# Sampled blocks of two batches counted through: full sets across a batch border, whole rows of two batches in one group

## The chip, the cores and the metric

The kernel runs on one core of a Trainium2 chip. The metric is the device time of one execution in microseconds (us), the median over several runs; lower is better.

## The reference

Block-sparse attention for 4 batches, 8 heads, 768 positions and a head width of 64, in blocks of 32 positions (24 blocks a batch), followed by a feed-forward with 512 inputs, 2048 hidden values and 512 outputs on all 3072 tokens. All numbers are float32.

```python
scores = scale * np.matmul(q, k.transpose(0, 1, 3, 2))
mask = np.abs(blk_i - blk_j) <= window                       # window = 1
mask = mask | (blk_i == 0) | (blk_j == 0) | (blk_i == n_blocks - 1) | (blk_j == n_blocks - 1)
for qb in range(n_blocks):
    for kb in sampled_blocks[qb]:                            # 3 blocks
        mask[qb*block:(qb+1)*block, kb*block:(kb+1)*block] = True
scores = np.where(mask, scores, -1e9)
attn = softmax(scores); x = attn @ v                         # x: tokens x 512
h = x @ w_in
out = (np.maximum(h, 0) + np.log1p(np.exp(-np.abs(h)))) @ w_out
```

So the query blocks 1 to 22 of a batch see at most eight key blocks: three neighbours, the first, the last, and three sampled ones. The query blocks 0 and 23 see all 24. The former are called sampled blocks here, the latter whole rows. The list of sampled blocks is the same for all batches.

## The kernel before

**Sets.** The attention works on sets of four query blocks (128 rows). The 24 blocks of a batch are taken in the order 1 to 23, then 0, and cut into six groups. Groups 0 to 4 hold 20 sampled blocks and are full sets. Group 5 holds the sampled blocks 21 and 22 and the whole rows 23 and 0; it is worked as two sets, first the whole rows (a "whole set"), then the two sampled blocks (a "half set", `ni = 2`). A batch has seven sets, the kernel 28. Each set has two units, of four heads each.

**A unit.** `scores` multiplies queries with gathered keys on TensorE (L579 for sampled blocks, one 64x32 corner of the array per block; L603 for whole rows) and adds the mask and takes the minimum on VectorE (L585, L610). `exponents` runs on ScalarE (L635). `transposes` turns the weights on TensorE (L648) and copies them out of PSUM (L653 VectorE, L655 ScalarE). `products` multiplies with the values (L687, L701). At the end of a set `normalise` divides by the sums (L717), and `turn`, `x_high` and `x_low` transpose the result and split it into a high and a low part for the feed-forward (L732, L746, L750). A set's output takes one of the 24 places of 128 tokens; three places make a tile of the feed-forward, eight tiles in all.

**Keys and values.** `kT` holds the keys of one batch in a single buffer. `gather_keys` copies from it into one of two buffers `kg`: the neighbours with one VectorE copy (L498), the first and last block with two ScalarE copies where the buffer still has those of another batch (L481), the sampled ones with three copies a block, on GpSimd apart from the first set (L512). After the scores of a batch's whole set, `score_piece` lets the remaining gathers of that batch be issued and asks for the next batch's keys (`load_kT`, four DMAs on SP's queue); gathers from the new keys follow three pieces later (`BEHIND`). The values come into one of two buffers: near ones by a DMA on SP's queue (L542), sampled ones by an indirect DMA a block from GpSimd (L545). Queries are loaded two groups ahead (`load_queries`, L448).

**Order.** Each unit is cut into two pieces, `score_piece` and `transpose_piece`, software-pipelined over units: scores run two units ahead of the values. There are 116 pieces. `needs` (L841) says how many of them must be done before tile t of the feed-forward can start: 15, 31, 43, 59, 71, 87, 99, 116. The first 15 run alone; after that `between` and `due` spread the others over the feed-forward's steps so that each tile's need is met half a step early.

**Feed-forward.** It runs in 128 steps (`hidden`, `project`), each with 12 matmuls of 384 columns (L238 to L240) and 9 of 512 (L296 to L298). In the first 48 steps all eight tiles meet the first six of sixteen slices of the weights; in the last 80 steps they meet the other ten. The attention lies beside the first 42 steps. Beside it `convert` also turns the 64-bit weights into 32-bit ones, in ticks that go by pieces and steps (ScalarE L156, L160; VectorE L166 to L183). `store` adds up and writes the output (L321 to L326).

Of the kernel before, what the change touches and what calls it, by code (L numbers as in the profile page):

```python
# [19 lines left out]
BLOCK = 32  # L20
# [30 lines left out]
def sparse_attention_ffn(  # L51
    ctx: ExitStack,
    tc: tile.TileContext,
    q: bass.AP,
    k: bass.AP,
# [20 lines left out]
    B, NG, P, NP, NI, _ = q.shape  # L76
    NB = k.shape[2]
# [16 lines left out]
    order = [(b, g) for b in range(B) for g in range(NG)]  # L94
    place = {bg: n for n, bg in enumerate(order)}
# [215 lines left out]
    def store(phase, t):  # L311
        for m in range(GROUPS):
            n = t * GROUPS + m
            b, g = order[n]
# [7 lines left out]
            lo = b * S + (4 * g + 1) * BLOCK  # L322
            n = P if g < NG - 1 else P - BLOCK
            nc.sync.dma_start(out=out[lo : lo + n], in_=os_[0:n])
            if n < P:
                nc.sync.dma_start(out=out[b * S : b * S + BLOCK], in_=os_[n:P])  # L326
# [7 lines left out]

    blk = ac.tile([P, NB * NR * 2], I32, name="blk")
    rf = ac.tile([P, NB, NR], F32, name="rf")
    pkf = ac.tile([1, NB], F32, name="pkf")
# [5 lines left out]
    ixf = ac.tile([P, NB], F32, name="ixf")  # L343
    ix = ac.tile([P, B, NB], I32, name="ix")
    mask = ac.tile([P, NG, NS], F32, name="mask")
    iu = ac.tile([P, NG], I32, name="iu")
    iuf = ac.tile([P, NG], F32, name="iuf")
    rp = ac.tile([P, NG, NR], F32, name="rp")
    hit = ac.tile([P, NG, NR], F32, name="hit")
    tmp = ac.tile([P, NG, NR], F32, name="tmp")  # L350
    zero = ac.tile([P, 1], F32, name="zero")
    nc.gpsimd.memset(zero, 0.0)
    for i in range(NI):
        nc.gpsimd.iota(
            iu[i * BLOCK : (i + 1) * BLOCK], pattern=[[NI, NG]], base=1 + i, channel_multiplier=0
        )
# [13 lines left out]
    nc.vector.memset(rp, 0.0)  # L370
# [34 lines left out]
    def make_mask():  # L405
        nc.vector.tensor_copy(out=iuf, in_=iu)

        for i in range(NI):
            rows = slice(i * BLOCK, (i + 1) * BLOCK)
            n = NG if i < 2 else NG - 1  # L410
            nc.vector.tensor_copy(out=rp[rows, 0:n], in_=rf[rows, 1 + i : 2 + i + NI * (n - 1) : NI, :])

        nc.vector.tensor_tensor(
            out=tmp, in0=rp, in1=iuf.unsqueeze(2).to_broadcast([P, NG, NR]), op=ALU.subtract
# [14 lines left out]
        nc.vector.memset(mask[0:BLOCK, 0, 0:1], NEG)  # L429
        nc.vector.memset(mask[BLOCK : 2 * BLOCK, NG - 1, 2:3], NEG)  # L430
# [12 lines left out]
    def load_queries(m):  # L443
        if m >= len(order):
            return
        b, g = order[m]
        qc[b, g] = wk.tile([P, NP, NI, BLOCK], F32, tag="qc", name=f"qc{b}_{g}", bufs=2)
        nc.sync.dma_start(out=qc[b, g], in_=q[b, g])  # L448
# [23 lines left out]
    def load_keys(*ms):  # L472

        wanted.extend(m for m in ms if m < len(order))
        while wanted and order[wanted[0]][0] in kT and not waiting:
            gather_keys(wanted.pop(0))

    def end_keys(m, copies):

        for copy, slot, blkno in zip(copies, (NR, 2 * NR + 1), (0, LAST)):  # L480
            copy(  # L481
                out=kg[m % 2][:, :, slot, :],
                in_=kT[order[m][0]][:, blkno : blkno + 1, :].to_broadcast([P, NI, NP * BLOCK]),
            )

    def gather_keys(m):
        b, g = order[m]
        ni = NI if g < NG - 1 else 2
        kd = kg[m % 2]

        def of_block(i):

            eng = (nc.vector if i < 2 else nc.scalar) if m == 0 else nc.gpsimd
            copy = nc.scalar.copy if m == 0 and i >= 2 else eng.tensor_copy
            if i == 0:
                at = kT[b][:, 4 * g : 4 * g + NR, :]
# [480 lines left out]
```

## Time and profile before

| | |
|---|---|
| median of 3 runs | 806.67 us (806.6 to 806.96) |
| profiled execution | 800.52 us, span of its instructions 798.7 us |
| TensorE matmul busy | 770.1 us, 96% of the span |
| TensorE weight loads busy | 645.6 us, 81% |
| VectorE busy | 536.4 us, 67% |
| ScalarE busy | 545.5 us, 68% |
| GpSimd busy | 188.2 us, 24% |
| DMA | 137.78 MB, mean 173 GB/s |

Busy times are averages over stages that have different limits, so they are read by stage below. TensorE's rows overlap, because matmuls are pipelined and small ones run beside each other; what a burst of them costs is read from the time at which it starts and the one at which the next work starts.

### The profile page before, as it was taken

Reading aid. Unit: us, or ns where it says so; the run is one execution under the profiler, and the core shown is the slowest. Engines: PE = TensorE matmul, PEld = TensorE weight load, DVE = VectorE, ACT = ScalarE, POOL = GpSimd, SP = SyncE. Lnnn points to the kernel's source line nnn. Section 1 sums busy time; section 2 is a strip of 40 time slices with the busy share of each in tenths; the row PEclk is TensorE's granted clock in tenths of the full one; section 3 lists DMA queues with packets and bytes.
Section 4 is the critical chain, followed back from the end, with each engine's and each line's share of the span. In section 5 each row is a group of like instructions: output and inputs, shape, how many; then the busy total and the mean of one; then the engine's idle time right before and its main releaser. Section 6 shows DMA issues by size and latency. Waiting matters only on the chain.

```text
span 798.7 us, 21332 instructions
## 1 busy us (share of the span) xinstructions
PE 770.1 (96%) x8108; PEld 645.6 (81%) x8108; DVE 536.4 (67%) x1379; ACT 545.5 (68%) x1306; POOL 188.2 (24%) x358
## 2 busy tenths in 40 slices
PE   8779999999999999999999999999999999999997
PEld 7556677777778777778788998899889988998896
DVE  5799999776878768776656864546454645455554
ACT  3798986867868678777667866555655565556553
POOL 6762955217345145442000000000000000000000
PEclk9999999999999999999999999999999999999999
DMA  7799787666767866857215922222130403021021
GB/s 289 274 349 348 256 295 272 236 232 234 288 229 271 311 252 221 282 165 260 97 41 185 355 81 79 80 77 83 34 125 1 146 14 139 20 107 53 0 80 41
DMA packets 42663, 137.78 MB, mean 173 GB/s; under 512 B 5248, under 2 KB 5376, under 8 KB 38080
## 3 DMA queue, kind: packets, MB, share of 16 engines
q1 hardware_dynamic: 35152, 112.15, 39.1%
q0 software_dynamic: 7120, 23.34, 8.0%
q8 instruction: 64, 1.05, 0.5%
q10 hardware_dynamic: 288, 0.93, 0.3%
q14 instruction: 39, 0.32, 0.1%
HBM read 105.98 MB, written 30.41 MB: 171 GB/s over the span
## 4 chain that ended last, share of the span: by engine, by line
PE 69%; DVE 12%; ACT 12%; issue 3%; DMA 2%; SPq 0%; POOL 0%; DVEq 0%; POOLq 0%; ACTq 0%
PE h L238 10%; PE o L296 10%; PE o L298 9%; PE o L297 9%; PE h L239 9%; PE h L240 9%; ACT pr L635 5%; PE x L687 3%; PE s L579 3%; PE t L648 3%; DVE pr L585 2%; PE warm L816 2%; DMA kT<-in_k_dram 2%; ACT pt L655 1%; DVE wt L179 1%
## 5 line engine op out<-in xcount | busy, mean ns | idle before, releaser
L253 DVE SCALAR_TENSOR_TENSOR e<-u,e 128x384 f32<-128x384 f32 x128 | 71.4, 558 | 177.3 <-ACT u L251 177.2
L238 PE MATMUL h<-x,w 128*128 128x384 f32 x512 | 178.3, 348 | 4.5 <-DVE nmax L610 2.5
L239 PE MATMUL h<-x,w 128*128 128x384 f32 x512 | 172.8, 338 | 0.0
L240 PE MATMUL h<-x,w 128*128 128x384 f32 x512 | 172.6, 337 | 0.0
L296 PE MATMUL o<-w,gh 128*128 128x512 f32 x384 | 156.0, 406 | 0.0
L297 PE MATMUL o<-w,gh 128*128 128x512 f32 x384 | 151.6, 395 | 1.2 <-issue 1.2
L298 PE MATMUL o<-w,gl 128*128 128x512 f32 x384 | 152.1, 396 | 0.0
L635 ACT ACTIVATE pr<-pr,nmax 128x256 f32<-128x256 f32 (+2 forms) x208 | 110.1, 531 | 59.4 <-DVE nmax L585 43.0
L244 ACT ACTIVATE e<-h 128x384 f32<-128x384 f32 x128 | 62.4, 488 | 117.3 <-PE h L240 117.3
L545 POOL DMA_INDIRECT vg<-in_v_dram,ix x88 | 92.0, 1046 | 117.0 <-PE x L687 90.8
L512 POOL COPY kg<-kT 128x128 f32 x252 | 93.1, 418 | 86.8 <-PE s L579 80.1
L238 PEld LDWEIGHTS h<-x,w 128*128 128x128 f32 x512 | 96.1, 188 | 19.3 <-DVE nmax L610 4.5
L239 PEld LDWEIGHTS h<-x,w 128*128 128x128 f32 x512 | 96.3, 188 | 4.9 <-issue 0.4
L240 PEld LDWEIGHTS h<-x,w 128*128 128x128 f32 x512 | 96.1, 188 | 0.0
L298 PEld LDWEIGHTS o<-w,gl 128*128 128x128 f32 x384 | 72.1, 188 | 19.0 <-issue 1.8
L268 ACT CAST gh<-u 128x384 fp32r<-128x384 f32 x128 | 65.6, 512 | 25.1 <-PE o L297 25.1
L296 PEld LDWEIGHTS o<-w,gh 128*128 128x128 f32 x384 | 72.1, 188 | 12.3 <-issue 0.8
L297 PEld LDWEIGHTS o<-w,gh 128*128 128x128 f32 x384 | 72.2, 188 | 10.7
L274 DVE TENSOR_TENSOR gl<-u,gh 128x384 fp32r<-128x384 f32 x128 | 70.6, 552 | 7.5 <-ACT gh L268 6.8
L585 DVE CUSTOM_DVE_ANT_1 pr<-s,mask 128x256 f32<-128x256 f32 (+1 forms) x192 | 70.0, 415 | 5.5 <-PE s L579 5.4
L259 ACT ACTIVATE u<-u 128x384 f32<-128x384 f32 x128 | 67.0, 523 | 9.3 <-DVE e L253 8.6
L254 DVE SCALAR_TENSOR_TENSOR e<-h,e 128x384 f32<-128x384 f32 x128 | 70.8, 553 | 2.7
(81 smaller groups left out, 1046.7 us busy)
## 6 DMA issues: line engine op xcount, KB each, us to landing
vg<-in_near_dram SPq DMA_DIRECT2D x19, 1024.0 KB, 5.3
xD<-x SPq DMA_DIRECT2D x8, 1536.0 KB, 6.0
x<-xD SPq DMA_DIRECT2D x8, 1536.0 KB, 7.3
raw<-in_w_in_dram SPq DMA_DIRECT2D x16, 512.0 KB, 7.2
raw<-in_w_out_dram SPq DMA_DIRECT2D x16, 512.0 KB, 9.3
qc<-in_q_dram SPq DMA_DIRECT2D x24, 256.0 KB, 6.1
vg<-in_v_dram SPq DMA_DIRECT2D x12, 512.0 KB, 6.5
yD<-os SPq DMA_DIRECT2D x24, 256.0 KB, 3.0
```

The source lines that it names most:

```text
L238: nc.tensor.matmul(ph, wh[:, cols], hi[:, c], start=(c == 0), stop=False)
L239: nc.tensor.matmul(ph, wh[:, cols], lo[:, c], start=False, stop=False)
L240: nc.tensor.matmul(ph, wl[:, cols], hi[:, c], start=False, stop=(c == NC - 1))
L253: nc.vector.scalar_tensor_tensor(out=e, in0=u, scalar=-1.0, in1=e, op0=ALU.add, op1=ALU.subtract)
L254: nc.vector.scalar_tensor_tensor(out=e, in0=ph, scalar=0.0, in1=e, op0=ALU.max, op1=ALU.subtract)
L296: nc.tensor.matmul(po[m], gh[:, cols], wh, start=first, stop=False)
L297: nc.tensor.matmul(po[m], gh[:, cols], wl, start=False, stop=False)
L298: nc.tensor.matmul(po[m], gl[:, cols], wh, start=False, stop=last)
L512: copy(out=kd[:, i, 1 + NR + s, :], in_=kT[b][:, bass.ds(x, 1), :].rearrange("p n f -> p (n f)"))
L545: nc.gpsimd.indirect_dma_start(out=vd[:, 1, i, :], out_offset=None, in_=v, in_offset=bass.IndirectOffsetOnAxis(ap=ix[:, b, 4 * g + 1 + i : ...
L585: nc.vector.tensor_tensor_reduce(out=pr[r][rows, j], in0=ps[r][rows, j], in1=mask[rows, g].unsqueeze(2).to_broadcast([ni * BLOCK, NS, BLOCK]),
L635: nc.scalar.activation(x, x, AF.Exp, bias=nmax[rows, r, j : j + 1], scale=-1.0, accum_out=rs[rows, h : h + 1])
```

## The change

The 22 sampled blocks of a batch are no longer cut into five and a half sets. The 88 sampled blocks of all batches are counted through in order and cut into 22 full sets; there is no half set any more. In each pair of batches (11 sets) the sixth set holds the blocks 21 and 22 of the first batch and 1 and 2 of the second.

- Whole rows stay one set a batch, but have their queries in an input of their own (`ends`) and stand now ahead of the fifth and the eleventh sampled set of a pair. Their normalised rows go to a tile `xe` that holds both batches; they are turned together, after the second one, and take one place of 128 tokens (`WHOLE`). There are 26 sets, 52 units, 108 pieces; `needs` becomes 15, 31, 43, 55, 67, 83, 95, 108.
- The keys of the middle set are gathered in two parts, one from each batch's keys. The first and last key block are copied for those block rows whose batch has changed (`stale`).
- The masks are made for the 11 sets of a pair instead of the 6 groups of a batch; since a set may have blocks of two batches, the block numbers are written for eight runs of blocks (`seams`) instead of four.
- The small tiles of the start lie in `xe`'s memory.
- `load_queries` counts sets instead of groups. `store` writes one DMA for each run of blocks that follow one another: one for most groups, two for a middle set, three for the whole rows.

```diff
+    spots = [(b, i) for b in range(B) for i in range(1, NB - 1)]
+    group = [spots[NI * j : NI * (j + 1)] for j in range(NM)]
+    PG = 2 * NM // B
+    WHOLE = PG - 2
+    def place(what, j):
+        pair, i = divmod(j, PG) if what == "s" else (j // 2, WHOLE)
+        return pair * (PG + 1) + i + (what == "s" and i >= WHOLE)
+    turns = {PG * pair + i: 2 * pair + w for pair in range(B // 2) for w, i in enumerate((NI, PG - 1))}
+    sets = []
+    for j in range(NM):
+        if j in turns:
+            sets.append(("w", turns[j]))
+        sets.append(("s", j))
...
+    xe = ac.tile([P, 2, DM // 2], F32, name="xe")
...
+    seams = [[j for j in range(PG) if group[j][i][0] == w] for w in range(2) for i in range(NI)]
+    seams = [(n % NI, js[0], js[-1] + 1, group[js[0]][n % NI][1]) for n, js in enumerate(seams)]
...
-        for i in range(NI):
+        for i, lo, hi, blk0 in seams:
             rows = slice(i * BLOCK, (i + 1) * BLOCK)
-            n = NG if i < 2 else NG - 1
-            nc.vector.tensor_copy(out=rp[rows, 0:n], in_=rf[rows, 1 + i : 2 + i + NI * (n - 1) : NI, :])
+            nc.vector.tensor_copy(
+                out=rp[rows, lo:hi], in_=rf[rows, blk0 : blk0 + NI * (hi - lo - 1) + 1 : NI, :]
+            )
...
+    def load_keys(*js):
+        for j in js:
+            if j < NM:
+                of = [b for b, _ in group[j]]
+                wanted.extend((j, b, of.index(b), of.index(b) + of.count(b)) for b in sorted(set(of)))
+        while wanted and wanted[0][1] in kT and not waiting:
+            gather_keys(*wanted.pop(0))
...
+    def gather_keys(j, b, lo, hi):
+        kd = kg[j % 2]
+        blk0 = group[j][lo][1]
+        stale = [i for i in range(lo, hi) if ended_in.get((j % 2, i)) != b]
+        for i in stale:
+            ended_in[j % 2, i] = b
...
-                if m % NG < 2:
-                    first = nc.vector.tensor_copy if m == 0 else nc.scalar.copy
-                    end_keys(m, (first, nc.scalar.copy))
+                if stale:
+                    rows = slice(stale[0], stale[-1] + 1)
+                    first = nc.vector.tensor_copy if j == 0 else nc.scalar.copy
+                    for end, slot, blkno in ((first, NR, 0), (nc.scalar.copy, 2 * NR + 1, LAST)):
+                        end(
+                            out=kd[:, rows, slot, :],
+                            in_=kT[b][:, blkno : blkno + 1, :].to_broadcast([P, len(stale), NP * BLOCK]),
+                        )
...
-            ni = NI if g < NG - 1 else 2
...
-                for i in range(ni):
+                for i in range(NI):
...
+        if what == "w":
+            xs = xe[:, j % 2]
...
+    def turns_now(m):
+        return m is not None and (sets[m][0] == "s" or sets[m][1] % 2 == 1)
...
-            if ended[1] is not None:
+            if turns_now(ended[1]):
                 turn(ended[1])
                 x_high(ended[1])
...
-            if scored is not None:
-                load_queries(scored + 2)
+            if queried is not None:
+                load_queries(queried + 2)
```

More of the change, by code (lines that the diff above doesn't have):

```diff
@@ L443, in load_queries @@
     def load_queries(m):
[L444 removed]
+        if m >= len(sets):
             return
[L446 to L448 removed]
+        what, j = sets[m]
+        at = wk.tile([P, NP, NI, BLOCK], F32, tag="qc", name=f"qc{m}", bufs=2)
+        if what == "w":
+            at = at.rearrange("p n i q -> p (n i q)")[:, 0 : NP * 2 * BLOCK]
+            at = at.rearrange("p (n i q) -> p n i q", n=NP, i=2)
+        qc[m] = at
+        nc.sync.dma_start(out=at, in_=ends[j] if what == "w" else q[j])
     regs = {}
@@ L470, in sparse_attention_ffn @@
     wanted, waiting = [], []
[L472 to L484, printed above, removed]
@@ L528, in load_values @@
             return
-        b, g, whole = sets[m]
+        what, j = sets[m]
         vd = vg[sets[m]] = vbuf[m % 2]
-        if whole:
+        if what == "w":
+            b = j
             rows = vd.rearrange("p c i f -> p (c i) f")
@@ L560, in scores @@
         m, a = units[n]
-        b, g, whole = sets[m]
+        what, j_ = sets[m]
+        whole = what == "w"
         st = state[n]
-        qd = qc[b, g]
+        qd = qc[m]
         nmax = st["nmax"] = wk.tile([P, 2, 2], F32, tag="nmax", name=f"nmax{n}", bufs=4)
@@ L621, in exponents @@
         m, a = units[n]
-        b, g, whole = sets[m]
+        whole = sets[m][0] == "w"
         st = state[n]
@@ L661, in values @@
         m, a = units[n]
-        whole = sets[m][2]
+        whole = sets[m][0] == "w"
         if a == NA - 1 and not whole:
@@ L670, in products @@
         m, a = units[n]
-        b, g, whole = sets[m]
+        whole = sets[m][0] == "w"
         pt = state[n]["pt"]
@@ L708, in normalise @@
     def normalise(m):
-        b, g, whole = sets[m]
+        what, j = sets[m]
         xq, rs = xps.pop(m), sums.pop(m)
-        rows = P if whole or g < NG - 1 else 2 * BLOCK
-        n = NP if whole else 2 * NP
-        xs = xss[m] = wk.tile([P, DM], F32, tag="xs", name=f"xs{m}")
-        rs = rs[0:rows, 0:n]
+        n = NP if what == "w" else 2 * NP
+        if what == "w":
+            xs = xe[:, j % 2]
+        else:
+            xs = xss[m] = wk.tile([P, DM], F32, tag="xs", name=f"xs{m}")
+        rs = rs[:, 0:n]
         nc.vector.tensor_scalar_add(out=rs, in0=rs, scalar1=1e-9)
@@ L750, in x_low @@
         nc.vector.tensor_tensor(out=lo, in0=src, in1=hi.bitcast(F32), op=ALU.subtract)
-        t, at = divmod(place[sets[m][:2]], GROUPS)
-        if not sets[m][2] and at == GROUPS - 1:
+        t, at = divmod(place(*sets[m]), GROUPS)
+        if at == GROUPS - 1:
             nc.sync.dma_start(out=xD[t], in_=X[0, t].bitcast(F32))
@@ L771, in score_piece @@
                 m, a = units[s]
-                b, g, whole = sets[m]
-                if whole and a == NA - 1 and b + 1 < B:
-                    gathered(key_work, place[b, g])
+                what, b = sets[m]
+                if what == "w" and a == NA - 1 and b + 1 < B:
+                    gathered(key_work, NM)
                     for n_ in range(4):
@@ L839, in sparse_attention_ffn @@
     attention = [piece for n in range(len(units) + 2) for piece in pieces(n)]
-    needs = [2 * sum(1 for m, a in units if place[sets[m][:2]] < (t + 1) * GROUPS) + 3 for t in range(NTB)]
+    needs = [
+        2 * max(n + 1 for n, (m, a) in enumerate(units) if place(*sets[m]) < (t + 1) * GROUPS) + 3
+        for t in range(NTB)
+    ]
     needs[-1] = len(attention)
```

193 lines of the change are left out of this document (97 added, 96 removed).

## The prediction

> **What bounds the kernel now.** I read first the stretches of the span, cut where the work changes: the attention alone, the attention mixed with the first feed-forward steps, and the feed-forward alone. The columns are the length, then busy time and instructions of TensorE, its weight loads, VectorE, ScalarE and GpSimd, the granted clock, the DMA share and GB/s.
>
> ```profile
> 14.86:57.70 42.84, 34.14 (x908) 23.42 (x908) 35.45 (x123) 33.60 (x101) 31.58 (x66) 0.96 0.80 299
> 57.70:135.00 77.30, 72.94 (x1098) 54.82 (x1093) 74.01 (x205) 67.26 (x176) 45.47 (x77) 1.00 0.81 296
> 135.00:240.00 105.00, 98.23 (x1538) 76.49 (x1524) 79.92 (x233) 77.45 (x207) 42.16 (x80) 1.00 0.68 246
> 240.00:420.00 180.00, 177.23 (x2621) 141.07 (x2620) 129.92 (x380) 132.80 (x352) 60.22 (x111) 1.00 0.60 211
> 440.00:720.00 280.00, 280.00 (x1401) 252.84 (x1400) 155.84 (x299) 172.54 (x348) 0.00 (x0) 1.00 0.27 96
> ```
>
> From 240 us on TensorE is busy without a gap worth naming and every other engine has a quarter of its time free: there the time is the sum of TensorE's instructions. From 135 to 240 us it is nearly so (94%). Between 57.7 and 135 us VectorE (74.01 of 77.30, 96%) is as full as TensorE (94%). Before 57.7 us no engine is full, and the stage runs on dependences and on the loads (80% DMA).
>
> Next, TensorE's own rows in time, because the page's mean duration of a matmul hides how many run at once. The columns are start, duration, line, shape, count; the first five rows are of full sampled sets, the others of the last half set and of the whole rows' set of batch 3.
>
> ```profile
> 219.19 1.09 PE L579 MATMUL s<-kg,qc 64*32 64x256 f32 x32
> 220.22 1.99 PE L687 MATMUL x<-vg,pt 128*32 128x64 f32 x128
> 372.86 1.09 PE L579 MATMUL s<-kg,qc 64*32 64x256 f32 x32
> 377.54 1.04 PE L648 MATMUL t<-ident,pr 128*128 128x128 f32 x8
> 399.36 0.60 PE L732 MATMUL y<-ident,xs 128*128 128x128 f32 x4
> ...
> 396.01 1.07 PE L579 MATMUL s<-kg,qc 64*32 64x256 f32 x16
> 402.60 1.07 PE L579 MATMUL s<-kg,qc 64*32 64x256 f32 x16
> 407.43 0.71 PE L648 MATMUL t<-ident,pr 64*128 64x64 f32 x8
> 411.34 0.38 PE L732 MATMUL y<-ident,xs 128*128 128x128 f32 x2
> 411.65 0.71 PE L648 MATMUL t<-ident,pr 64*128 64x64 f32 x8
> 413.53 1.98 PE L687 MATMUL x<-vg,pt 128*32 128x64 f32 x64
> ```
>
> This is the row pair that decides: a half set has half the score records (16 against 32) and half the value records (64 against 128), and takes the same time for them (1.07 against 1.09 us, 1.98 against 1.99 us). The records of the four 32-column groups run beside each other; with two blocks, two of the four places stand empty.
>
> **The change part by part.**
>
> *The sets.* Before, each pair of batches has 10 full, 2 half and 2 whole sets; after, 11 full and 2 whole. A full set on TensorE is two score bursts, two transpose bursts, one value burst and one turn: 2 x 1.09 + 2 x 1.04 + 1.99 + 0.60 = 6.85 us. A half set: 2 x 1.07 + 2 x 0.71 + 1.98, and its turn, which is four transposes of 64 columns and which I estimate at 0.5 (between the 0.38 and the 0.60 of the y rows): 6.04 us. A pair loses two half sets and gains one full: 2 x 6.04 - 6.85 = 5.2 us, and both pairs 10.5 us. A check of the 6.85:
>
> ```profile
> 340.86:356.23 15.37, 3.02 (x8) 1.50 (x9) 1.00 0.55 173
> 440.00:720.00 280.00, 89.90 (x267) 49.94 (x266) 1.00 0.27 96
> ```
>
> These stretches count line L238 alone, of which a feed-forward step has four. In the pure stage one costs 280 / 267 = 1.049 us of time; the 15.37 us that hold one full set between two chunk starts hold 8 of them, 8.39 us, which leaves 6.98 us for the set. So the bursts' sum is what a set costs, chopping of the feed-forward included.
>
> The Trainium skill says otherwise of how to judge this engine: Perfetto Trace Analysis, Identifying the Most-Contended Engine, calls matmul busy time a bad measure and takes the share of the weight loads instead. What that would make of the change is the second rival below.
>
> *ScalarE and VectorE.* Per half set they do nearly a full set's work, since their time goes by columns and not by partitions:
>
> ```profile
> L635 ACT ACTIVATE pr<-pr,nmax 128x256 f32<-128x256 f32 x160 | 79.5, 498 | 42.0 <-DVE nmax L585 41.9
> L635 ACT ACTIVATE pr<-pr,nmax 64x256 f32<-64x256 f32 x32 | 15.8, 495 | 1.2 <-DVE nmax L585 1.2
> L585 DVE CUSTOM_DVE_ANT_1 pr<-s,mask 128x256 f32<-128x256 f32 x160 | 58.3, 416 | 4.6 <-PE s L579 4.6
> L585 DVE CUSTOM_DVE_ANT_1 pr<-s,mask 64x256 f32<-64x256 f32 x32 | 11.7, 410 | 0.9 <-PE s L579 0.7
> L498 DVE COPY kg<-kT 128x1536 f32<-128x1536 f32 x20 | 20.4, 1020 | 0.0
> L653 DVE COPY pt<-t 128x512 f32<-128x512 f32 x28 | 19.0, 679 | 1.8 <-PE t L648 1.8
> L750 DVE TENSOR_TENSOR x<-y,x 128x512 fp32r<-128x512 f32 x20 | 13.7, 684 | 9.5 <-ACT x L746 9.5
> L750 DVE TENSOR_TENSOR x<-y,x 128x256 fp32r<-128x256 f32 x8 | 3.4, 419 | 3.0 <-ACT x L746 2.9
> L498 DVE COPY kg<-kT 128x768 f32<-128x768 f32 x4 | 2.3, 582 | 0.0
> L653 DVE COPY pt<-t 128x256 f32<-128x256 f32 x4 | 1.7, 417 | 2.5 <-PE t L648 2.5
> ```
>
> So 16 exponents (16 x 0.5 = 8 us of ScalarE) and 16 masked reductions (16 x 0.41 = 6.6 us of VectorE) go. From 135 us on that is off the path. In the stretch where VectorE is full, the count of pieces up to a given step is unchanged (both kernels run 15 pieces ahead and 16 in the next 5.5 steps, counted through the loops), so there the first half set is replaced by a full one and the saving comes later: VectorE pays (1020 - 582) + (679 - 417) + (684 - 419) = 0.97 us in place of TensorE's 0.81. I add 0.2 us.
>
> *The whole rows.* Their scores, exponents and values stay. Two turns of two transposes (0.38 each) become one of four (0.60): 0.16 us a pair, 0.3 us in all. The four separate loads of their queries stand on SP's queue two sets ahead of their use, as the others do: nothing. If SP were late by one of them, a score burst would wait for up to its landing time (last column), which I keep inside the reload's bounds below.
>
> ```profile
> qc<-in_q_dram SPq DMA_DIRECT2D x24, 256.0 KB, 6.1
> ```
>
> *The start.* The masks get four more copies of the sampled numbers and two more memsets, all on VectorE ahead of the first keys:
>
> ```profile
> 8.60 0.84 DVE L411 COPY rp<-rf 32x18 f32<-32x18 f32 x4
> 12.38 0.06 DVE L430 MEMSET mask<- 32x1 f32 x1
> 12.45 1.19 DVE L498 COPY kg<-kT 128x1536 f32<-128x1536 f32 x1
> 14.86 1.11 PE L579 MATMUL s<-kg,qc 64*32 64x256 f32 x12 [0.45 <-issue]
> 26.07 2.89 issue
> ```
>
> 4 x 0.21 + 2 x 0.06 = 1.0 us. The copy at 12.45 and the first scores at 14.86 follow at once, so the upper bound is 1.0. But at 26.07 the chain of waits has 2.89 us in the middle of the first set's values, whose loads don't hang on the masks; that could swallow all of it. Between 0 and 1.0 I take 0.5. Four more index fills on GpSimd end before the sampled numbers land: nothing.
>
> *The reload of the keys.* One buffer holds the keys of a batch, so the next batch is loaded when the last reader is done. The chain shows what it costs at the first two borders:
>
> ```profile
> 72.52 6.25 DMA kT<-in_k_dram
> 178.47 6.43 DMA kT<-in_k_dram
> ```
>
> Counted through the loops, the reload is asked for and first needed at these steps: before 1.25 to 3.25, 12.67 to 15.0, 24.67 to 27.0; after 0 (in the stage ahead of the feed-forward) to 2.0, 11.25 to 14.25, 23.25 to 25.5. The second border gets 0.67 steps more of lead, the others the same. What waits behind the reload is larger now: the middle set of a pair takes its second half's keys from the new batch, with a copy on VectorE, two on ScalarE and six on GpSimd, each in its engine's order ahead of exponents and feed-forward work. No run shows this set. The bounds are a whole reload gained (-6.4) and one lost (+6.3); since the second border's lead grows and the others don't change, I take -1.0.
>
> GpSimd must copy that set's first half before the reload. The half set's six copies stood at the same place in its order, so it is not later.
>
> *The end.* The last group's output left in two transfers, now in one:
>
> ```profile
> 795.32 0.33 SPq L324 DMA_DIRECT2D out_dram<-y  x1
> 795.70 0.43 SPq L326 DMA_DIRECT2D out_dram<-y  x1
> ```
>
> The second is issued 0.4 us after the first: I take -0.3. The whole rows' three short transfers are the first of that tile and end under the others.
>
> *Sum.* -10.5 + 0.2 - 0.3 + 0.5 - 1.0 - 0.3 = -11.4 us. The profiled execution has a span of 798.7 and a time of 800.52 us; it would come to 787.3 and 789.1. The runs' median lies 6.15 us above the profiled time; I take the difference over to it: 806.67 - 11.4 = 795.3.
>
> One more rule speaks against the change: TensorE: Matmul & The Clock Gate, What's actually happening, in the Trainium skill, halves the clock after an idle window of about 3.4 us. The whole rows now run with no feed-forward work to fill their waits. The trace agrees where it can: the stretch with the 2.89 us wait has a granted clock of 0.96. By the rule one such window more would cost an estimated 1.7 us, and the sum would be -9.7.
>
> **The rivals.**
>
> *The first pair gives nothing* (13%). Ahead of 240 us VectorE, ScalarE and the loads set the pace, and shorter TensorE work is only waited out. For it: VectorE's 96%, and idle TensorE before 57.7. Against: the saving falls at 135 to 240 us, where TensorE has 94% and VectorE 76%. Then 5.2 us of the sum are gone: 800.5.
>
> *TensorE pays by weight loads* (10%). The half sets' score and value loads number as many after as before. 64 transposes of half sets and their 16 of the turn go, 32 full ones and 8 of the turn come:
>
> ```profile
> L648 PEld LDWEIGHTS t<-ident,pr 128*128 128x128 f32 x416 | 47.3, 142 | 14.6 <-issue 3.1 <-DVE e L254 2.1 <-ACT pr L635 1.9
> L648 PEld LDWEIGHTS t<-ident,pr 64*128 64x128 f32 x64 | 4.7, 138 | 2.1 <-issue 1.2 <-PE h L240 0.3 <-PE t L648 0.2
> ```
>
> 80 x 0.138 - 40 x 0.142 = 5.4 us, in place of 10.5, gives 800.4. Against it stand the equal bursts at 396 and 372 us. This is what the rule of the Trainium skill cited above would give.
>
> *The middle set waits* (7%, slower). The keys' reload for it is asked for at the end of the whole rows, in the first pair among the loads at 80% DMA. If it lands a full reload late, in-order ScalarE stands still with the exponents behind it, 6.25 and 6.43 us in the two pairs: 12.7 more than counted, 808.0. It decides from 5.7 us a middle set on. At just that price no change is left (4%). Against it: the lead in steps is the same as today's.
>
> *The reloads vanish* (6%). If the longer lead covers a whole border's 6.4 us, beyond the 1.0 counted, the time is 789.9.
>
> **How the numbers follow.** The forecast has 60%, with its own range 791.5 to 799. The range for 8 in 10 takes in the two rivals at 800.5 and the bound of the reload below: 789.5 to 803. A measurement of this kernel can tell about 0.2% (1.6 us) from no change. Faster: 60 + 13 + 10 + 6 = 89%; same 4%; slower 7%.
>
> **What would show it.** TensorE's score bursts all x32, none x16; in the stretches from 135 us on, the stage ending some 10 us earlier with the same busy share. Line L635 at 192 instead of 208, L648 at 448 instead of 480. A first score burst about 1 us later. A chain whose reload rows are at most two of 6 us. The prediction is wrong if the middle sets' score bursts follow a wait of over 5 us, or if the pure feed-forward begins less than 5 us earlier.

## The result and the profile after

The changed kernel takes 800.41 us, the median of 20 runs (795.24 to 807.93); the kernel before took 804.80 us beside it, also the median of 20 (801.49 to 806.96). The ratio is 0.9942, with a 95% interval of 0.9929 to 0.9955: about 4.7 us faster; it leaves out the 807.93, an execution in a slower state. The forecast was 11.4 us faster.

The profiled execution of the changed kernel took 804.06 us, 3.7 above its median; that of the kernel before took 800.52 us, less than any of the 20. So the two profiles lie 3.5 us apart the wrong way, and some 8 us of what differs between them belongs to these two executions and not to the change. I compare them stage by stage, and say beside the stages that lose what other profiles of the two kernels show there.

What the change does to the instructions is as foretold. The groups of the changed kernel by line and shape (busy time and mean ns of one, then idle time before it):

```profile
L674 ACT ACTIVATE pr<-pr,nmax 128x256 f32<-128x256 f32 x176 | 87.4, 498 | 44.7 <-DVE nmax L625 44.5
L674 ACT ACTIVATE pr<-pr,nmax 128x768 f32<-128x768 f32 x16 | 14.9, 930 | 22.6 <-DVE nmax L656 22.6
L687 PE MATMUL t<-ident,pr 128*128 128x128 f32 x448 | 63.3, 279 | 10.6 <-DVE nmax L625 2.8 <-issue 2.6 <-DVE e L274 2.3
L619 PE MATMUL s<-kg,qc 64*32 64x256 f32 x1408 | 55.1, 393 | 4.4 <-issue 1.5 <-POOL kg L560 1.2 <-DVE e L274 0.5
```

The exponents (now line L674) number 176 + 16 = 192, the transposes (L687) 448, and no exponent and no transpose of 64 partitions is left. Yet the time fell by less than half of the sum.

To see where, I cut both profiles at the same places of the program: first scores, first feed-forward matmul, and the starts of feed-forward steps 6, 22, 34 and 42, a step being twelve matmuls of the three h lines, counted in the trace. Attention's last set ends with step 42. The kernel before, then the changed one (columns as in the prediction's first view):

```profile
14.86:57.73 42.87, 34.17 (x908) 23.42 (x909) 35.48 (x125) 33.63 (x101) 31.58 (x66) 0.96 0.80 299
57.73:116.06 58.33, 54.64 (x806) 40.76 (x802) 55.40 (x155) 51.74 (x135) 34.45 (x58) 1.00 0.82 299
116.06:259.12 143.06, 135.62 (x2092) 106.25 (x2090) 114.15 (x328) 109.55 (x292) 64.49 (x118) 1.00 0.70 255
259.12:364.44 105.32, 103.09 (x1583) 81.14 (x1582) 81.82 (x238) 80.84 (x217) 45.83 (x89) 1.00 0.71 246
364.44:426.63 62.19, 61.65 (x795) 49.98 (x794) 35.27 (x105) 39.53 (x99) 3.09 (x4) 1.00 0.38 134
```

```profile
15.95:58.95 43.00, 35.88 (x876) 23.17 (x876) 36.88 (x127) 33.13 (x96) 28.88 (x60) 0.96 0.78 280
58.95:122.55 63.60, 55.22 (x931) 42.27 (x928) 56.70 (x156) 54.04 (x142) 36.05 (x68) 0.95 0.82 307
122.55:256.99 134.44, 130.22 (x1977) 102.18 (x1976) 106.54 (x298) 101.67 (x267) 56.77 (x108) 1.00 0.69 251
256.99:372.93 115.94, 107.21 (x1677) 84.13 (x1676) 84.94 (x241) 83.47 (x220) 47.35 (x88) 0.97 0.68 240
372.93:429.13 56.20, 56.11 (x681) 45.84 (x680) 31.89 (x84) 34.37 (x80) 3.79 (x4) 1.00 0.37 136
```

The stages don't hold the same work in both kernels. By their value matmuls (tile `vg`; a half set has 64, a full one 128), a half set is gone from steps 6 to 22 (992 for 1056) and from 34 to 42 (352 for 416), and a half set has become a full one in steps 0 to 6 (480 for 416) and 22 to 34 (864 for 800). By the prediction's 6.04 and 6.85 us a set that should make -6.0, -6.0, +0.8 and +0.8 us.

Two stages gain as the sum had it or more: steps 6 to 22 give 143.06 - 134.44 = 8.6 us and the last one, 34 to 42, gives 62.19 - 56.20 = 6.0. Two stages lose: steps 0 to 6, around the first reload of the keys, lose 5.3, and steps 22 to 34 lose 10.6, where TensorE has 8.7 us of idle time instead of 2.2 and a granted clock of 0.97 instead of 1.00. The start is 1.1 us later.

The loss of 5.3 us is partly chance: in the profiles of this study that keep the reloads and ScalarE's copies, steps 0 to 6 take 58.3 to 61.8 us in the kernel before and 61.0 to 63.6 in the changed one. The loss of 10.6 us is not: steps 22 to 34 take 113.7 to 117.6 us in all five profiles of the changed kernel and its variants with the stream unmoved, and 105.3 to 107.7 in five of six of the kernel before (the sixth, 112.8, is met below).

The chain of waits of the changed kernel (start, length, what) shows what stands in the two losing stages:

```profile
27.45 2.38 issue
47.22 1.40 issue
57.90 11.41 DMA kT<-in_k_dram
69.33 0.41 ACT kg L549
...
275.20 7.63 DMA kT<-in_k_dram
303.85 0.64 issue
319.16 0.87 issue
335.23 2.63 issue
337.86 1.04 PE t L687 x5
338.90 0.43 PE o L316
```

In the first, a reload row of 11.41 us, where before had 6.25 us (7.6 from the first of its four DMAs, with which the row of 11.41 begins), and behind it ScalarE's copy of the end blocks (L549). In the second, waits named "issue", which the page explains as time in which an engine waited for nothing that the profile shows. They stand inside bursts: the one at 335.23 us cuts eight transposes of one PSUM tile into three and five. The clock falls behind such waits:

```profile
73.30:79.70 6.40, 6.33 (x87) 4.81 (x87) 5.21 (x16) 5.85 (x12) 3.91 (x13) 0.57 0.47 184
335.24:337.85 2.61, 0.00 (x0) 0.00 (x0) 2.26 (x6) 1.64 (x5) 2.15 (x4) 1.00 1.01 318
337.86:341.25 3.39, 3.39 (x11) 2.82 (x12) 1.72 (x3) 1.19 (x3) 2.65 (x3) 0.55 0.95 341
```

For 3.4 us behind the wait, and for 6.4 us behind the reload, TensorE ran at a little over half clock; the o matmul at 338.90 us takes 0.43 us of the chain where the same ones take 0.23 at full clock. The DMA share during the wait is 1.01: every engine of the DMA was busy.

### The profile page after: what moved, and what is told of

Same layout as the page of the kernel before. It is cut to its first block, busy times and chain, and to the rows that moved or that the text cites. A ratio compares the mean times of both kernels' runs of the same rounds, so it can differ in the third digit from the quotient of the medians.

```text
span 802.2 us, 21194 instructions
## 1 busy us (share of the span) xinstructions
PE 766.7 (96%) x8068; PEld 642.8 (80%) x8068; DVE 532.2 (66%) x1340; ACT 537.4 (67%) x1268; POOL 183.3 (23%) x362
## 4 chain that ended last, share of the span: by engine, by line
PE 72%; DVE 11%; ACT 10%; DMA 4%; issue 3%; SPq 0%; DVEq 0%; ACTq 0%
PE h L258 10%; PE o L316 10%; PE h L259 10%; PE o L318 10%; PE h L260 10%; PE o L317 10%; ACT pr L674 4%; PE s L619 3%; PE x L723 3%; PE t L687 3%; DMA kT<-in_k_dram 2%; PE s L643 2%; DVE pr L625 2%; ACT pt L692 1%; DVE wt L199 1%
## 5 line engine op out<-in xcount | busy, mean ns | idle before, releaser
L674 ACT ACTIVATE pr<-pr,nmax 128x256 f32<-128x256 f32 (+1 forms) x192 | 102.3, 534 | 67.3 <-DVE nmax L625 44.5
L560 POOL COPY kg<-kT 128x128 f32 x252 | 90.4, 405 | 104.0 <-PE s L619 87.8
L586 POOL DMA_INDIRECT vg<-in_v_dram,ix x88 | 89.3, 1015 | 103.2 <-PE x L723 78.0
L288 ACT CAST gh<-u 128x384 fp32r<-128x384 f32 x128 | 65.6, 513 | 25.5 <-PE o L317 25.5
L687 PE MATMUL t<-ident,pr 128*128 128x128 f32 x448 | 63.3, 279 | 10.6 <-DVE nmax L625 2.8
L284 DVE TENSOR_TENSOR u<-u,e 128x384 f32<-128x384 f32 x128 | 70.9, 554 | 1.8 <-ACT u L279 0.2
```

Of the source, the lines that this page charges most:

```text
L560: copy(out=kd[:, i, 1 + NR + s, :], in_=kT[b][:, bass.ds(x, 1), :].rearrange("p n f -> p (n f)"))
L586: nc.gpsimd.indirect_dma_start(out=vd[:, 1, i, :], out_offset=None, in_=v, in_offset=bass.IndirectOffsetOnAxis(ap=ix[:, b, blk_ : blk_ + 1 ...
L674: nc.scalar.activation(x, x, AF.Exp, bias=nmax[:, r, j : j + 1], scale=-1.0, accum_out=rs[:, h : h + 1])
L687: nc.tensor.transpose(ps[:, i], st["pr"][r][:, c * P : (c + 1) * P], ident)
```

## The experiments

### Without the reloads

```
 def load_part(b, lo, hi, engine):   # both kernels
+    if b > 0:
+        kT[b] = kT[0]
+        return
```

> The kernel before, leaving out the reload of the keys: batches 1 to 3 use the keys of batch 0, so nothing waits at a batch border, and the rest is the same. It sets the base for the next run. Both theories: the two visible border waits of before (stalls of 3.4 us around 71 to 85 us and 2 to 3 us around 188 us on TensorE) go, so the ratio to before is about 0.993 to 0.995 (4 to 5 us less).

> The changed kernel, leaving out the same reload. Theory A (the sets' saving on TensorE is there, and what is missing was lost at the borders between batches): with no border to wait at, the changed kernel is 10 us (9 to 11.5) faster than the kernel before without its reload, so about 0.981 of before. Theory B (TensorE saves only by its weight loads, 5.4 us; the borders cost both kernels the same): it is 5 us faster than that, about 0.987 of before. Theory C (what is short of VectorE and ScalarE ahead of 240 us eats the first pair): 5 us as well, but the difference is made after 240 us alone.

Measured, beside 805.01 us for before: 799.65 us without reloads in the kernel before (ratio 0.9939, 0.9921 to 0.9957), 795.10 us in the changed one (0.9894, 0.9861 to 0.9928). The reloads cost the kernel before 5.4 us and the changed one 800.41 - 795.10 = 5.3 us (3.9 by the ratios). In the profiles their price only moved: before, the stage of steps 0 to 6 lost 58.33 - 57.08 = 1.3 us by them and steps 6 to 22 lost 143.06 - 139.55 = 3.5; after, steps 0 to 6 lose 63.60 - 58.06 = 5.5 and steps 6 to 22 nothing. And between the two kernels without reloads lie only 4.6 us, not ten. So theory A, which put the whole loss at the borders, falls: something else eats 5 to 6 us. Theories B and C foretold just such a distance. C also wants all of it made after 240 us, and that is not so: without reloads steps 6 to 22 gain 139.55 - 134.77 = 4.8 us, of the 6.0 that a half set should give (the kernel before, then the changed one). B is met below, by the doubled half sets.

```profile
115.27:254.82 139.55, 134.95 (x2091) 105.86 (x2090) 112.92 (x326) 109.03 (x290) 62.32 (x121) 1.00 0.68 249
117.29:252.06 134.77, 129.95 (x1977) 102.00 (x1976) 105.88 (x298) 102.81 (x270) 57.96 (x114) 1.00 0.66 237
```

In steps 22 to 34 the changed kernel without reloads still is at a clock of 0.98 and 8.3 us longer than its counterpart (105.45 us):

```profile
252.06:365.79 113.73, 105.80 (x1677) 82.97 (x1676) 84.41 (x241) 82.28 (x217) 46.48 (x83) 0.98 0.66 230
```

### ScalarE kept out of the border, and the X write held back

```
-  for end, slot, blkno in ((first, NR, 0), (nc.scalar.copy, 2 * NR + 1, LAST)):
+  last = nc.scalar.copy
+  if j > 1:
+      first = last = nc.gpsimd.tensor_copy
+  for end, slot, blkno in ((first, NR, 0), (last, 2 * NR + 1, LAST)):
```

> The changed kernel with the copies of the first and last key block made by GpSimd in place of ScalarE, apart from the first two sets. In the changed kernel's trace such a copy stands on ScalarE at 69.3 us, waits for the keys, and the exponents behind it hold up a burst of transposes for 5.2 us, after which TensorE's clock is halved for some 4 us. Theory A1 (it is the place in ScalarE's order that costs): the burst's stall falls below 2 us, the clock stays up, and the time falls by 4 to 7 us against the changed kernel, to about 0.987 of before. Rival A2 (the keys themselves land too late, the scores of the middle set wait instead): the stall moves to the middle set's score burst and the time stays at 0.994.

Measured 799.51 us, ratio 0.9938 (0.9916 to 0.9961): no difference from the changed kernel, so the 4 to 7 us of theory A1 did not come. Steps 0 to 6 did shrink, from 63.60 to 60.08 us in its profile, since ScalarE no longer stands behind the reload; but steps 22 to 34 stayed at 117.58 us.

```
-  nc.sync.dma_start(out=xD[t], in_=X[0, t].bitcast(F32))
+  if t in (0, 2, 4):
+      held.append([t, HOLD])      # issued three score pieces later
+  else:
+      nc.sync.dma_start(out=xD[t], in_=X[0, t].bitcast(F32))
```

> The changed kernel with the write of the finished feed-forward input tiles 0, 2 and 4 (1.5 MB each) issued three pairs of pieces later, behind the reload of the keys. In the changed kernel this write is issued 1.2 us ahead of the reload, which then takes 11.4 us; before, the write went 16 us ahead of it, and the reload took 6.25 us. Theory A2 (the write and the reload share the DMA engines): the reload lands in 6 to 8 us, the stall of the transposes falls below 2 us, and the time falls by 4 to 7 us against the changed kernel. Rival (the other loads of that stage, at 80% DMA, hold the reload up): it still takes over 10 us, and the time stays at 0.994 of before.

Measured 802.89 us, ratio 0.9975 (0.9946 to 1.0003): no gain, if anything a loss. Its chain shows a first reload row of 7.07 us, which begins with the fourth DMA of the reload; from the first one, at 56.70 us, it is 9.1 us, against 11.4 with the 1.5 MB write of X issued 1.2 us ahead. So the write did lengthen the reload, by some 2 us in these two profiles. But the time does not hang on it. Steps 0 to 6 took 61.92 us, within what other profiles show, and steps 22 to 34 took 115.67 us. Why the median is not lower, this profile (of 801.45 us) doesn't show.

```profile
58.77 7.07 DMA kT<-in_k_dram
```

### The place in the stream of instructions

All four profiles of the changed kernel and its variants had a wait of 2.6 to 3.0 us at the same transposes (in one of them put down to VectorE). I numbered TensorE's instructions (matmuls, weight loads and its sequencer's semaphores) in order of their starts, and set the waits that lay beside a transfer of the instruction queue (16 KB each, which makes 64 bytes for each of 256 instructions) against that number. Worked out from the changed kernel's trace:

```
wait at us   length   number   = 256 x n + place   transfer began, against the wait's start
   27.45      2.38      705        2, 193              -0.31
   47.22      1.40     1472        5, 192              -0.81
  319.16      0.87     9664       37, 192              -1.34
  335.23      2.63    10177       39, 193              +0.34
```

In the chains of waits of the seventeen profiles of this study, all 55 rows "issue" of 1 us or more stand at place 192 to 194 of 256, and TensorE goes on 2.2 to 2.8 us after the transfer began. That is theory F of the texts below: TensorE runs out of instructions. To test it, the whole stream is moved by extra matmuls during the warm-up; nothing else changes.

```
   for n in range(WARM):
       nc.tensor.matmul(warm[:, n % 4], ident, ident, start=True, stop=True)
+  for n in range(32):      # or 64
+      nc.tensor.matmul(warm[:, n % 4, 0:16], ident, ident[:, 0:16], start=True, stop=True)
```

> The changed kernel with 32 more warming matmuls of 16 columns at the start, so that every later TensorE instruction stands 64 places further on in the engine's stream and nothing else moves. Theory F (TensorE now and then runs out of instructions at fixed places of its stream, next to a 16 KB instruction transfer, and runs at half clock behind the wait): the wait of 2.6 to 3.0 us that all four profiles of the changed kernel have at the same transposes (335.23 us in its own profile) vanishes or turns up at another instruction, and the time moves by 2 to 6 us, most likely down, to about 797. Rival R (that wait belongs to what the kernel does there: its exponents, its copies, the PSUM buffers): the wait stays at the same transposes with 2.5 to 3 us, and the time is 800 to 802.

> The same with 64 such matmuls, so 128 places. Theory F: again another pattern of waits, none of over 2 us at the same transposes; the time differs from that of the kernel with 32 by up to 5 us either way, the longer start aside (at most 2 us). Rival R: the wait stays, the time is 801 to 803 because the start is longer.

> The kernel before with the same 32 matmuls. Theory F: its waits (2.89 us at 26 us in the first set's values, about 1.2 us at 225 us) move or change, and the time moves by up to 4 us either way; as it has no such wait in its second half, it is more likely to lose (806 to 808). Rival R: the same waits at the same instructions, the time within 1.5 us of before.

Two things were not as I had thought. Each of these matmuls is two in the stream, each with its weight load: 32 of them move it by 128 places in place of 64, and 64 of them by 256, one whole block. The page of the changed kernel with 32, whose count was x8068 without:

```profile
PE 771.1 (96%) x8132; PEld 649.0 (81%) x8132; DVE 531.6 (66%) x1340; ACT 536.5 (67%) x1268; POOL 182.0 (23%) x362
```

And the first scores come late, at 24.12 us in both kernels with 32 and at 37.79 us with 64, in place of 15.95 and 14.86. The timeline of the changed kernel with 32, and the stretch cut at 19 us:

```profile
14.81 9.38 PE L860 MATMUL warm<-ident 128*128 128x16 f32 x62
24.12 1.51 PE L619 MATMUL s<-kg,qc 64*32 64x256 f32 x21
```

```profile
14.81:19.00 4.19, 4.19 (x41) 4.19 (x39) 1.86 (x7) 0.00 (x0) 3.73 (x10) 1.00 0.62 222
19.00:24.10 5.10, 5.10 (x26) 5.08 (x25) 0.00 (x0) 0.00 (x0) 1.96 (x3) 0.52 0.63 201
```

From 19 us on the clock is halved, though TensorE has no gap: 26 of these matmuls take 5.10 us there, where 41 took 4.19 us before.

The medians are 802.39, 821.12 and, for the kernel before, 816.20 us. With the later start taken off (8.17, 21.84 and 9.26 us) they are 794.2, 799.3 and 806.9. So half a block takes 6 us off the changed kernel (800.41), a whole block changes little (1.1 us), as a stream that repeats every 256 should have it, and half a block adds 2 us to the kernel before (804.6 in that comparison). The wait at the transposes is gone with 128 places and back with 256, at number 10,433, which is 40 x 256 + 193. The timeline of the kernel with 256:

```profile
351.98 0.49 PE L687 MATMUL t<-ident,pr 128*128 128x128 f32 x3
355.10 0.77 PE L687 MATMUL t<-ident,pr 128*128 128x128 f32 x5 [2.63 <-issue]
```

The same three and five, the same 2.63 us. A wait of the program would have stayed with 128 places; this one did not, so theory F stands and its rival falls. Where the second text looked for another pattern of waits, it had the wrong number of places.

### The price of a half set

```
-  for i in range(ni):
+  for i in range(NI):                     # scores, and the same in the values
-      ps[r][32*i : 32*i+32, j], qd[half, p, i, :], kd[half, i, :, cols],
+      ps[r][32*i : 32*i+32, j], qd[half, p, i, :], kd[half, i % ni, :, cols],
```

> The kernel before, whose half sets do their score and value matmuls twice: the second time into the two empty 32-partition places, from the same blocks (output rows that nothing reads); 384 records more. By the rows from which the forecast was made (a burst of 16 score records took 1.07 us, one of 32 took 1.09; 64 value records 1.98, 128 took 1.99) four half sets cost 4 x (2 x 0.02 + 0.01) = 0.2 us more: 805. If TensorE pays by records, 4 x (2 x 1.07 + 1.98) = 16.5 us more: 821, and the forecast's 10.5 us never was there.

Measured 809.60 us, ratio 1.0053 (1.0027 to 1.0080): 4.3 us more, near neither number. The last stage, steps 34 to 42, tells them apart, for there nothing else waits:

```profile
373.80:436.06 62.26, 61.72 (x892) 50.16 (x890) 35.39 (x105) 39.54 (x99) 3.09 (x4) 1.00 0.37 134
```

It has 97 matmuls more than before (892 against 795) and is 0.07 us longer. By the first row pair of the prediction 96 records of one half set add 0.05; by records they would have added 4.1. So theory B, and with it a price by records or by weight loads, falls. The rest lies ahead of step 26 (in the profile, which is 9.4 us longer than that of before, all but 0.1 us does), beside other waits at place 193 (4.25 us at 55.81 us, number 1,985), since each doubled half set moves all that follows by 192 instructions.

### Both kernels at other places

The next kernels replace 8 warming matmuls by narrow ones (128x32 by 128x64, quick), and add more of them. The first four texts still count two places for each extra matmul, where there are four: "116 places" are 232, and "88" are 176.

```
-WARM = 50
+WARM = 42
+  for n in range(66):      # 66, 52, 66, 8 in the first four, then 36, 30, 36
+      rows = slice(n % 4 * BLOCK, (n % 4 + 1) * BLOCK)
+      nc.tensor.matmul(warm[rows, n // 4 % 4, 0:64], ident[:, rows], ident[:, 0:64], start=True, stop=True)
```

> The changed kernel with 8 warming matmuls fewer and 66 narrow ones (128x32 by 128x64) more, so that all later TensorE instructions stand 116 places further on. In the profiles so far each wait of over 0.8 us with no releaser named, if it stands beside an instruction transfer, is at place 192 to 194 of 256 in the engine's stream, and TensorE goes on 2.2 to 2.7 us after that 16 KB transfer began. Theory F (these waits are the instructions' and depend on which bursts of short matmuls come ahead of such a place): the profile of the changed kernel, moved by 116, has 7 stretches shorter than 7 us ahead of such places in place of 10, and their lack sums to 6.7 us in place of 14.2; the time falls by 5 to 9 us, to 792 to 796, and the wait at 335 us is gone. Rival R (waits of the program): 800, with up to 1 us for the longer start.

> The kernel before with 8 warming matmuls fewer and 52 narrow ones more: 88 places further on, where the same sum falls from 12.5 to 4.2 us (none of it after 60 us). Theory F: the time falls by 4 to 8 us, to 797 to 801, and the changed kernel at its good place stays 6 to 11 us faster than this one: that is then what the change is worth beside the instructions. Rival R: 805 to 806.

> The changed kernel with the end copies of the later batches on GpSimd, and the same 116 places: Theory F: 791 to 796, within 2 us of the changed kernel so moved; rival R: 799.5.

> The changed kernel with 8 warming matmuls replaced by 8 narrow ones: nothing is moved. Both theories: 800 to 801, with the wait at about 335 us at the same transposes. Were it faster by over 2 us, fewer warming matmuls would be the cause of what the moved kernels show, and not their places.

Measured, beside 805.59 us for before: the unmoved control 802.54 us (ratio 0.9975, 0.9947 to 1.0002), with its wait of 2.65 us at 335.37 us; the changed kernel at 232 places 797.53 us (0.9912, 0.9884 to 0.9940); with GpSimd's end copies besides 794.52 us (0.9881, 0.9843 to 0.9919), the fastest kernel of this study, though its interval overlaps those of the other moved ones. Five us between the control and the moved kernel come from places alone. The 797.53 us lie above the 792 to 796 of the text, which were worked out for another place. The kernel before at 176 places went the other way, to 812.60 us (1.0113, 1.0075 to 1.0151), where I had expected 797 to 801. For the 176 places at which it really stands, the text on 88 places below works out waits of 14.5 us, against 11.1 unmoved. Its steps 22 to 34 took 112.8 us. Its timeline, with a wait of 4.08 us at number 10,176, three matmuls short of the end of a value burst, and half clock behind it:

```profile
328.81 1.90 PE L687 MATMUL x<-vg,pt 128*32 128x64 f32 x121
334.80 0.42 PE L687 MATMUL x<-vg,pt 128*32 128x64 f32 x3 [4.08 <-issue]
335.15 0.69 PE L238 MATMUL h<-x,w 128*128 128x384 f32 x1
```

With the count mended, three more:

> The changed kernel with 8 warming matmuls fewer and 36 narrow ones more, each of them two in TensorE's stream: all later instructions stand 112 places further on. Worked out from the trace (the time of the 320 instructions ahead of each place 192 of 256, against the delay that instruction transfers had at that point of the program in the profiles so far, plus 2.4 us): waits of 6.8 us in all, 0.5 of it after 60 us, where the changed kernel unmoved has 12.8 and 5.0. Theory F: 793 to 796, no wait of over 1 us at 304, 320 and 335 us, and the clock no longer halved behind them. Rival R (the waits do not depend on places): 800 to 802.

> The kernel before with 8 warming matmuls fewer and 30 narrow ones more: 88 places further on. By the same working waits of 6.5 us in all, none after 60 us (unmoved 11.1 and 1.5; at 176 places 14.5 and 8.9, where 16.7 and 8.4 were seen). Theory F: 802 to 804.5, so 7 to 10 us behind the changed kernel at its good place: the sets' saving is there and the places covered it. Theory G (the saving is only some 4 us, the noreload pair's difference): at most 5 us behind the changed kernel.

> The changed kernel with the later batches' end copies on GpSimd, 112 places further on. Theory F: 791 to 795; as the end copies made no difference unmoved (799.5 against 800.4), within 2 us of the changed kernel at 112 places. Rival R: 799 to 801.

Measured, beside 804.58 us for before: 796.26 us for the changed kernel (0.9901, 0.9877 to 0.9926), 807.07 us for the kernel before (1.0029, 1.0007 to 1.0052), 795.59 us for the changed one with GpSimd's end copies (0.9900, 0.9873 to 0.9926). The changed kernel's stages:

```profile
15.85:60.79 44.94, 35.41 (x877) 23.42 (x877) 37.07 (x128) 33.23 (x96) 29.07 (x60) 0.96 0.80 292
60.79:122.52 61.73, 53.92 (x932) 41.25 (x929) 56.45 (x156) 54.01 (x142) 35.63 (x68) 0.97 0.80 291
122.52:257.60 135.08, 130.28 (x1978) 102.19 (x1977) 106.39 (x298) 101.59 (x267) 56.70 (x108) 1.00 0.71 253
257.60:365.96 108.36, 104.98 (x1678) 82.80 (x1677) 84.28 (x241) 83.12 (x220) 47.85 (x88) 0.98 0.72 256
365.96:422.16 56.20, 56.11 (x682) 45.84 (x681) 31.89 (x84) 34.37 (x80) 3.79 (x4) 1.00 0.39 138
```

Steps 22 to 34 fell from 115.94 to 108.36 us with the same instructions, and steps 6 to 22 and 34 to 42 are within 0.7 us of what they were. Its chain has no wait named "issue" of 0.8 us or more after 102 us; one of 1.77 us at 101.67 us was not foretold. The distance between the kernels at their new places is 807.07 - 796.26 = 10.8 us, a little over what theory F expected and far from theory G's five; at 128 places it was 806.9 - 794.2 = 12.7. But that is not yet what the sets are worth: 2.5 us of the 10.8 are a loss of the kernel before at its new place. Against the kernel before unmoved, the best place that it had in these runs, the moved changed kernel gains 804.58 - 796.26 = 8.3 us. What failed is the forecast for the kernel before, 802 to 804.5: its late waits went, as worked out, but its early ones grew. Its stage of attention alone and its chain:

```profile
14.72:63.70 48.98, 38.22 (x913) 25.93 (x909) 36.81 (x127) 34.44 (x107) 31.85 (x66) 0.86 0.75 284
```

```profile
25.27 3.52 issue
39.37 2.64 issue
54.11 1.31 issue
60.23 2.29 issue
```

So the rule tells where such waits can stand and that TensorE goes on 2.2 to 2.8 us after the transfer's start; how late a transfer starts, above all early on, it doesn't tell well enough for a forecast of a few us.

## Why the prediction was right and wrong

*What bounds the kernel.* "From 240 us on ... the time is the sum of TensorE's instructions": this is the step that failed. It holds for what the semaphores order. It leaves out that the instructions themselves must be there: in the changed stream other bursts of short matmuls stand at the places of a block at which TensorE can run out, and steps 22 to 34 lost 10.6 us where a set more should cost 0.8. Moving the stream gave 7.6 us of that back in the profiles, and 4.1 us between the medians (800.41 and 796.26). The prediction's own sign of being wrong came as well: step 42, behind which the feed-forward is alone, started at 429.13 us in place of 426.63. The 2.89 us at 26.07 us, which the prediction quoted and put into the first set's values, was such a wait: it stands at number 705, as it does in the changed kernel.

*The sets, -10.5.* Right, where the stages let it be seen. The last stage, which loses one half set, gave 6.0 us for the 6.04 of the sum, and doubled half sets cost 0.07 us there; without reloads steps 6 to 22 gave 4.8 for the other half set, and steps 0 to 6 cost 58.06 - 57.08 = 1.0 for the 0.8. In steps 22 to 34 even the moved kernel takes 3.0 us more than before (108.36 against 105.32), not 0.8. From step 6 to step 42 the kernel before took 143.06 + 105.32 + 62.19 = 310.57 us; the changed one took 306.58 as it stands and 135.08 + 108.36 + 56.20 = 299.64 at its other place. Over that stretch the gain is 4.0 us unmoved and 10.9 us moved; some 3.5 of it is the second border's reload, which no longer costs anything (see below).

*The start, +0.5.* Mis-sized: 14.86 became 15.95 us and the first feed-forward matmul 57.73 became 58.95. It is the upper bound, 1.0, and a little more; nothing swallowed it.

*The reload, -1.0.* Nothing came of it: 5.4 us in all before, 5.3 after. The longer lead did hide the second border's, but the first border took 11.41 us, where it cost 5.5 us in place of 1.3: SP now issues a 1.5 MB write 1.2 us ahead of the reload (with the write held back it took 9.1 us from its first DMA), and ScalarE's copies stand behind it.

*VectorE's +0.2 and the whole rows' -0.3* can't be told apart in these profiles. *The end, -0.3:* wrong, it is about +1.0. From the start of step 42 to TensorE's end both kernels take 367.9 us. But from there to the end of the span the kernel before takes 798.7 - 794.57 = 4.1 us and the changed one 802.2 - 797.07 = 5.1 (4.1 to 4.4 and 4.9 to 5.1 in all profiles). The prediction counted one transfer for two in the last group, and said that the whole rows' three would end under the others. They stand ahead of the last groups on SP's queue, which now issues five transfers there in place of four. It is done with them 798.94 - 797.07 = 1.9 us after TensorE, where it was 796.13 - 794.57 = 1.6 (last matmul of before, then last matmul and transfers of the changed kernel; the transfers of before are in the prediction):

```profile
794.17 0.40 PE L298 MATMUL o<-w,gl 128*128 128x512 f32 x1
796.67 0.40 PE L318 MATMUL o<-w,gl 128*128 128x512 f32 x1
796.42 2.52 SPq L344 DMA_DIRECT2D out_dram<-y  x5
```

What makes up the rest of the 1.0 us stays open.

*The clock-gate sentence.* It gave one idle window 1.7 us. The Trainium skill's rule (TensorE: Matmul & The Clock Gate, What's actually happening) halves the clock after an idle window of about 3.4 us, and the trace agrees that the clock halves: 0.55 behind a wait of 2.61 us, 0.57 behind the first border. But these waits need not be as long as that window, for the clock also fell behind a wait of 1.28 us. That one stands among the whole rows' scores, which wait for VectorE:

```profile
261.31 0.86 PE L643 MATMUL s<-kT,qc 64*64 64x384 f32 x4 [1.28 <-DVE nmax L650]
263.11:266.52 3.41, 3.41 (x15) 3.02 (x14) 0.31 (x1) 3.41 (x9) 0.00 (x0) 0.50 0.47 184
```

So the half-clock window that the prediction feared for the whole rows is there, near 260 us in seven of eleven profiles of the changed kernel and its variants, in the moved one too, and in none of the kernel before. It is no wait for instructions, and 3.41 us at half clock lose 1.7 us, as the sentence had it. By the chain, six o matmuls of 0.43 in place of 0.23 us, the five transposes and the first h matmul make some 1.5 us for the wait at 335 us, beside its own length.

*The rivals.* Two of them gave 800.5 and 800.4, where the time came out, and neither is the reason. The first pair does give: steps 6 to 22 gained 8.6 us, and 4.8 without the reloads. TensorE does not pay by weight loads: 96 loads more beside the half set's own cost 0.07 us. The middle set's wait is half there: ScalarE did stand behind the first reload (keeping it out took 3.5 us off that stage), but in the second pair steps 22 to 34 stayed long without ScalarE's copies too (117.58 us). The reloads did not vanish.

Put together: 800.41 us is what the changed kernel does at the place that the change happened to give it; at other places of its stream it takes 794.2, 797.5 and 796.3 us. That these lie around the forecast of 795.3 is in part luck. The forecast started from 806.67 us, where the kernel before later measured 804.80; as a ratio it was 0.9859, and the two moved kernels whose start is not late have 0.9912 and 0.9901. Of the 6.7 us between 0.9859 and 0.9942, 0.9942 to 0.9901 is 3.3 us of places. The reload's missing 1.0, the end's 1.3 and the start's 0.6 make 2.9 more. That is bookkeeping and no proof, since the moved kernel has waits for instructions of its own in the attention alone (44.94 us there against 42.87).

What stays open: what makes one instruction transfer late and the next not. The DMA share was 1.01 in the wait at 335 us, which speaks for the bulk loads, but no run took these away alone.

## What to carry to other kernels

Where a sum says that an engine is busy without a gap, look in the chain for waits named "issue" inside a burst, number the engine's instructions and see whether these waits stand at one place of a block: then a change that only shortens the stream also moves it, and a move alone changed the medians by 1 to 7 us here, down for the changed kernel and up for the kernel before. Before a change of one per cent is judged, run both kernels with their streams moved by half a block and compare at more than one place. Count the moved instructions in the trace, not in the code.

## What the runs showed of the hardware

- TensorE's instructions come in 16 KB transfers of 256 (63 transfers for 16,273 recorded instructions of the changed kernel), and it can run dry: waits of up to 4.25 us, at place 192 to 194 of a block, ending 2.2 to 2.8 us after a transfer's start. The Trainium skill (Runtime: NRT & Kernel Launch, Instruction fetch mechanics) says that the cost of crossing such a block is mostly hidden. In the feed-forward alone the trace agrees: a transfer every 25.5 us or so there, and no such wait. In the mixed stage it does not, and the measurement decides.
- The mean granted clock of a run goes with its time: the changed kernel took 795.24 us at 0.998 and 804.06 us at 0.987. A straight line through its 20 runs has 0.76 us for each 0.001 of clock (correlation -0.90), where 0.001 of 800 us is 0.8.
- A 16-column warming matmul of 128x128 weights was two in the stream. These took 4.19 us / 41 = 0.10 us each at full clock and 5.10 / 26 = 0.20 at a granted clock of 0.52, which came in a stretch where TensorE had no gap.
